# Turning ten units' last keys by VectorE blocks and a DRAM trip in place of TensorE, in a gated linear attention followed by four experts

## The chip, the cores and the metric

The kernel runs on one core of one Trainium2 chip, as one program. The metric is device time in microseconds, from the first to the last instruction of a launch as the device reports it; lower is better. A core has a matrix engine (TensorE, called PE in the profile, with its weight loads as PEld), VectorE (DVE), ScalarE (ACT), GpSimd (POOL) and SyncE (SP), which here only issues DMAs. Each engine runs its own instructions in order, and engines wait for each other with semaphores. SBUF and PSUM are the on-chip memories, with 128 partitions each; DRAM is off the core.

## The reference

A recurrence over 768 tokens for 4 batches and 8 heads of width 48, and then a mixture of four two-layer experts on the rows it makes:

```python
state = np.zeros((B, H, D, D))                       # B, H, S, D = 4, 8, 768, 48
for t in range(S):
    state = alpha[:, :, t, :, None] * state + np.einsum('bhd,bhe->bhde', k[:, :, t], v[:, :, t])
    y[:, :, t] = np.einsum('bhd,bhde->bhe', q[:, :, t], state)
x = y.transpose(0, 2, 1, 3).reshape(B * S, H * D)    # 3072 x 384
p = domain_probs / (domain_probs.sum(-1, keepdims=True) + 1e-09)
for e in range(4):                                   # w1[e]: 384 x 1024, w2[e]: 1024 x 384
    out += p[:, e:e + 1] * (np.maximum(x @ w1[e], 0.0) @ w2[e])
```

All is float32.

## The kernel before

**Units.** The attention is cut into 24 units of 128 tokens: six blocks of tokens (`cb`) by four batches (`b`), numbered u = 0 to 23 with the batch running fastest. Tokens of a unit are worked on all at once. The decays inside a unit are applied in seven doubling levels: at level li, queries in the later half of each block of 2^(li+1) tokens are multiplied by the decay up to them, keys in the earlier half by the decay after them, and TensorE multiplies the two (`products`). After the seventh level the keys (`KTs[-1]`) carry the decay up to the unit's last token, and keys times values is what the unit adds to the running state `st` of its batch.

**Layouts.** In the working layout of keys, queries and decays, a partition is one of 64 padded channels of one of two heads of a pair, and along a partition lie 4 pairs by 128 tokens. From the third unit on (u >= 2), rows are loaded in runs so that VectorE can turn them into that layout with its own 32x32 block transposes (`turn`, L444). To multiply keys by values over tokens, the keys must lie with tokens on partitions. That last turn is made by TensorE, four 128x128 turns into PSUM (`turned`, L246), and a ScalarE copy from there into the tile `AT` (L658). `AT` held the decays until then and is free.

**Steps.** `attention(u)` is a generator of 17 steps:

| step | what is emitted |
|---|---|
| 0, 1, 2 | decays, keys and queries turned (L444); then the loads of the next unit's rows on SP's queue (L161, L165, L170, L171) |
| 3 to 10 | the levels: `copy_q` (ACT, L508), `next_q` and `next_k` (DVE, L515, L517, L529; ACT, L528), `products` (PE, L536), `take` (DVE, L546) |
| 11 | the products of the far half (PE, L602), the last products and takes, `next_k(6)` (DVE) |
| 12, 13 | the scores copied into `lat` (ACT: L615 in step 12, L619 in step 13) |
| 14 | `turn_keys`: the last keys turned (PE, L246) and copied to `AT` (ACT, L658) |
| 15 | `result`: scores times values and queries times state (PE, L641, into `yps`), copied out by ACT and DVE (L653, L654) |
| 16 | keys times values (PE, L672, into `sps`), the state updated (DVE, L680 to L683), the values of unit u + 2 loaded (SP, L165) |

**Experts.** Units form groups, the first of two units, the rest of four, save the last. For each group and expert, `up` runs the first layer (PE, L728, into `one`; ACT L730 and DVE L753 take it out of PSUM as two parts, a coarse one and the rest), and `down` the second (PE, L797, into `ops`; L821 or L823 adds it up). Weights are split in the same way once, written to DRAM (`kept`, L221) and read back piece by piece for each later group (L195 on SP's queue, 768 KB a piece, four pieces a layer). A first-layer piece is read again as soon as its last use has been emitted, and two of four second-layer pieces (`late`) after the first piece of the next `up`.

**Order.** The order on every engine is written out by hand. `deal` gives each step of each unit a due time within the time of the expert work before the unit's group is wanted; a unit takes two unit spaces (some 39 us each), so that two units are under way at once. The steps' places in that time are the fractions in `IN_PAIRS` for units 11 to 17 (`in_pairs`) and in `BEATS` for the others. `advance` adds up the costs that `cost` gives for the expert work, and emits the steps that have come due between two matmuls. Due times are not changed by what a step holds.

The names that matter below: `by_pairs` is 10, and `in_rows` holds for u >= 10. `keys()` gives a tile from the five buffers of `KT`. `NP` is 4 pairs, `P` 128, `QUAD` 32, `NTOK` 4, `D` 48, `HD` 64, `NCB` 6. `apart_` tells whether the key-value product is made for each head by itself (64 columns by 48) or for two heads at once (128 by 96, of which half is used). `dram` is a pool of DRAM tiles. `rv` holds the unit's values with tokens on partitions.

Of the kernel before, what the change touches and what calls it, by code (L numbers as in the profile page):

```python
# [10 lines left out]
F32 = mybir.dt.float32  # L11
# [9 lines left out]
def kernel(  # L21
# [11 lines left out]
    nc = tc.nc  # L33

    B, H, S, D = q.shape
    E, DM, F = moe_w1.shape
    P = 128
    NCB = S // P
    NP = H // 2
    HD = 64  # L40
    QUAD = 32
# [12 lines left out]
    n = np.arange(QUAD)[None, :]  # L54
# [10 lines left out]
    dram = ctx.enter_context(tc.tile_pool(name="dram", bufs=1, space=bass.MemoryType.DRAM))  # L65
# [32 lines left out]
    NTOK = P // QUAD  # L98
# [14 lines left out]
    def raw(u, nm):  # L113
        if nm == "v":
            return values[u % 2]
        return rows_of[nm][:, 0] if u >= in_runs else apart[nm] if u == 1 else early[nm]
# [16 lines left out]
    in_pairs = range(half + 2 * B + 1, half + 4 * B)  # L133
# [106 lines left out]
    def halves(t, m):  # L240
        return t.rearrange("p a (b two r) -> p a b two r", two=2, r=m)

    def turned(src):
        tp = ps.tile([P, NP, P], F32, name="tp", tag="w")
        for p in range(NP):
            nc.tensor.transpose(tp[:, p, :], src(p), ident)  # L246
        return tp
# [171 lines left out]

    def rest_of_first(AT, KT, rv):  # L420
        nc.scalar.copy(out=AT, in_=turned(lambda p: KT[:, p, :]))
        yield
        sps = ps.tile([P, NP, 2, D], F32, name="sps", tag="w")
        for p in range(NP):
            nc.tensor.matmul(sps[:, p], lhsT=AT[:, p], rhs=rv[:, 2 * p:2 * p + 2, :D], start=True, stop=True)
        for i in range(2):
            rows = slice(HD * i, HD * (i + 1))
            nc.vector.tensor_copy(out=sts[units[0][1]][rows, :, i, :], in_=sps[rows, :, i, :])
        load(2, "v")
        yield  # L430

    def attention(u):
        cb, b = units[u]
        ra, rk, rq, rv = (raw(u, nm) for nm in ("a", "k", "q", "v"))
        pair = lambda t: lambda p: t[:, 2 * p:2 * p + 2, :].rearrange("p b c -> p (b c)")
        keys = lambda: work.tile([P, NP, P], F32, name="KT", bufs=5)

        AT = work.tile([P, NP, P], F32, name="AT")
        QT = work.tile([P, NP, P], F32, name="QT")

        def turn(nm, out):
            t = runs_of[nm]
            t = bass.AP(tensor=t.tensor, offset=t.offset, ap=[list(t.ap[0]), [RUN, NP], [D, NTOK], [1, QUAD]])
            nc.vector.transpose(out=out.rearrange("p a (t n) -> p a n t", n=NTOK), in_=t)  # L444
# [7 lines left out]
        in_rows = u >= by_pairs  # L452
        if in_rows:
            nc.gpsimd.tensor_mul(rows_of["q"][:, 1], rows_of["q"][:, 1], rows_of["a"][:, 0])
        yield
        KT = keys()
        if u >= in_runs:
            nc.scalar.activation(out=AT, in_=AT, func=ACT.Copy, scale=ident_all[:, P + HALF:P + HALF + 1])  # L458
            turn("k", KT)
        else:  # L460
            nc.scalar.copy(out=KT, in_=turned(pair(rk)))
        dot = work.tile([P, 2, H], F32, name="dot", bufs=1)
# [33 lines left out]
        KTs = [KT]  # L496
# [23 lines left out]
        def next_k(li):  # L520
            m = LEVELS[li]
            old = new = halves(KTs[li], m)
            if li == 0 and in_rows:
                KTs.append(KT)
            elif li + 1 < len(LEVELS):
                KTs.append(keys())
                new = halves(KTs[-1], m)
                nc.scalar.copy(out=new[:, :, :, 1, :], in_=old[:, :, :, 1, :])  # L528
            nc.vector.tensor_mul(new[:, :, :, 0, :], old[:, :, :, 0, :],  # L529
                                 spread(halved(decs[li])[:, :, :, 1], m))  # L530
# [11 lines left out]
        def take(li, scores):  # L542
            m = LEVELS[li]
            nb = HALF // (2 * m)
            mk = masks[:, li, :].rearrange("p (b r) -> p b r", r=m)
            nc.vector.copy_predicated(  # L546
                near.rearrange("p a (b two r) -> p a b two r", two=2, r=m)[:, :, :, 1, :],
                mk.unsqueeze(1).broadcast_to([P, H, nb, m]),
                scores.rearrange("p a (b r) -> p a b r", r=m))
# [50 lines left out]
        for r in range(NP // 2):  # L600
            for s in range(2):
                nc.tensor.matmul(far[HALF * s:HALF * (s + 1), r],  # L602
                                 lhsT=KTs[6][:, 2 * r + s, :HALF], rhs=qbs[6][:, 2 * r + s],
                                 start=True, stop=True)
# [3 lines left out]
        take(4, bank[:, 0])  # L608
        take(5, bank[:, 1])
        next_k(6)  # L610
        yield
        parts = lat.rearrange("p (r s i) c -> p r s i c", s=2, i=2)
        for s in range(2):
            rows = slice(HALF * s, HALF * (s + 1))
            nc.scalar.copy(out=parts[:HALF, :, s, :, HALF:], in_=far[rows])  # L615
        yield
        for s in range(2):
            rows = slice(HALF * s, HALF * (s + 1))
            nc.scalar.copy(out=lat[rows, :, rows], in_=near[rows])  # L619
        KT = KTs[-1]  # L620
        yield

        st = sts[b]
# [30 lines left out]
            nc.vector.tensor_sub(low, yps, top.bitcast(F32))  # L654

        def turn_keys():
            if cb < NCB - 1:
                nc.scalar.copy(out=AT, in_=turned(lambda p: KT[:, p, :]))  # L658


        for step in (turn_keys, result) if u >= half else (result, turn_keys):
            step()
            yield

        if cb < NCB - 1:
            KB = AT
            apart_ = u + 1 in in_pairs
            sps = ps.tile([P, NP, 1 if apart_ else 2, D], F32, name="sps", tag="w")
            for p in range(NP):
                for i in range(2) if apart_ else [slice(0, 2)]:  # L670
                    rows = slice(HD * i, HD * (i + 1)) if apart_ else slice(0, P)
                    nc.tensor.matmul(  # L672
                        sps[rows, p], lhsT=KB[:, p, rows],
                        rhs=rv[:, 2 * p + i, :D] if apart_ else rv[:, 2 * p:2 * p + 2, :D],
                        start=True, stop=True)
            for i in range(2):
                rows = slice(HD * i, HD * (i + 1))
                old, add = st[rows, :, i, :], sps[rows, :, 0 if apart_ else i, :]
                if cb == 0:
                    nc.vector.tensor_copy(out=old, in_=add)  # L680
                else:
                    nc.vector.tensor_mul(old, old, decs[-1][rows].broadcast_to([HD, NP, D]))
                    nc.vector.tensor_add(old, old, add)  # L683
# [159 lines left out]
    def deal():  # L843
# [14 lines left out]
        for gis in [*([gi] for gi in range(1, LAST - 1)), [LAST - 1, LAST]]:  # L858
# [6 lines left out]
            for k in range(n):  # L865
                u = sum(map(len, groups[:gi])) + k
                end = due - (n - 1 - k) * space
                begin = max(end - 2 * space, ends[-2])
                ends.append(end)
                run = attention(u)  # L870
                pairs = u in in_pairs
                beats = [0.0, *(IN_PAIRS if pairs else BEATS)]
                due_at = {-1: begin, **{j: begin + (end - begin) * beats[j + 1] for j in (7, 11, 16)}}
                for ahead, j in TOGETHER if pairs else ():
                    if (u > in_pairs[0] or j == 11) and abs(times[-1][ahead] - due_at[j]) < space / 6:
                        due_at[j] = times[-1][ahead]

                marks = sorted(due_at)
                times.append([])
                for lo, hi in zip(marks, marks[1:]):  # L880
                    times[-1] += [due_at[hi] if j == hi else
                                  due_at[lo] + (due_at[hi] - due_at[lo]) * (beats[j + 1] - beats[lo + 1])
                                  / (beats[hi + 1] - beats[lo + 1]) for j in range(lo + 1, hi + 1)]

                for j, ahead in ((6, 13), (12, 15)):
                    if times[:-1]:
                        times[-1][j] = max(times[-1][j], times[-2][ahead] + 0.5)
                events += [(time, u, run) for time in times[-1]]
# [8 lines left out]
    with tc.manual_schedule():  # L897
# [22 lines left out]
        def fill(times, n=P):  # L920
            for _ in range(times):
                nc.tensor.matmul(idle[:, :n], lhsT=zeros[:, :P], rhs=zeros[:, :n], start=True, stop=True)

        runs = [None, attention(1)]
        fill(7)
        runs[0] = first_unit(fill, runs[1])
# [56 lines left out]
```

## Time and profile before

| what | us |
|---|---|
| median of 3 runs (lowest to highest) | 1003.51 (1002.51 to 1006.27) |
| the profiled execution: time, span of its instructions | 1003.91, 1002.1 |
| DVE block turn L444, 128x512, mean of one (AT, KT, QT) | 1.10, 1.10, 1.10 |
| PE turn L246, 128x128, mean of one | 0.273 |
| ACT copy L658, 128x512 out of PSUM, mean of one | 0.585 |
| DMA to landing, median: `w<-kept` 768 KB, `sa` 88 KB, `out_dram<-acc` 192 KB | 6.8, 2.3, 2.3 |

The granted TensorE clock is 0.999 of full speed over the span. Landing times are counted from the issue, so a DMA behind others in its queue shows a longer one. On PE, f32 matmuls leave two records each, matmuls in the reduced f32 format (`fp32r`) one.

The units' places in the span, from the timeline: far products (step 11) of units 10, 11, 12, 17, 18, 19 start at 325.9, 351.6, 392.2, 588.2, 643.2 and 676.6 us; their key-value products (step 16) at 351.1, 391.7, 430.9, 625.3, 664.8 and 697.8 us. The first layer of an expert starts at 317.6, 359.4, 398.6, ... 632.8, 672.4 us, the second at 338.2, 379.7, 418.9, ... 651.0, 694.4 us.

### The profile page before, as it was taken

Reading aid. Unit: us, or ns where it says so; the run is one execution under the profiler, and the core shown is the slowest. Engines: PE = TensorE matmul, PEld = TensorE weight load, DVE = VectorE, ACT = ScalarE, POOL = GpSimd, SP = SyncE. Lnnn points to the kernel's source line nnn. Section 1 sums busy time; section 2 is a strip of 40 time slices with the busy share of each in tenths; the row PEclk is TensorE's granted clock in tenths of the full one; section 3 lists DMA queues with packets and bytes.
Section 4 is the critical chain, followed back from the end, with each engine's and each line's share of the span. In section 5 each row is a group of like instructions: output and inputs, shape, how many; then the busy total and the mean of one; then the engine's idle time right before and its main releaser. Section 6 shows DMA issues by size and latency. Waiting matters only on the chain.

```text
span 1002.1 us, 20402 instructions
## 1 busy us (share of the span) xinstructions
PE 979.5 (98%) x8244; PEld 869.9 (87%) x8244; DVE 572.2 (57%) x1188; ACT 407.2 (41%) x886; POOL 51.8 (5%) x94
## 2 busy tenths in 40 slices
PE   8799899999999999999999999999999999999998
PEld 7667678988989889889899899898898999999997
DVE  5688878476776555665645646756676521222222
ACT  5667656454452542523533413345344322111111
POOL 2000001000011000000000000000000000000000
PEclk9999999999999999999999999999999999999999
DMA  8898989595976774955946849759767405060611
GB/s 182 269 290 216 297 279 361 165 315 138 320 213 215 253 231 135 294 191 167 323 137 210 253 153 261 245 138 301 233 174 252 158 1 217 36 220 34 222 47 32
DMA packets 182798, 204.95 MB, mean 205 GB/s; under 512 B 110608, under 2 KB 159120, under 8 KB 182704
## 3 DMA queue, kind: packets, MB, share of 16 engines
q1 hardware_dynamic: 176240, 173.79, 57.8%
q0 software_dynamic: 6016, 29.49, 7.5%
q8 instruction: 65, 1.06, 0.4%
q10 hardware_dynamic: 448, 0.36, 0.1%
q14 instruction: 29, 0.24, 0.1%
HBM read 173.72 MB, written 29.88 MB: 203 GB/s over the span
## 4 chain that ended last, share of the span: by engine, by line
PE 84%; DVE 7%; ACT 4%; issue 2%; DMA 2%; SPq 1%; POOL 1%; DVEq 0%; ACTq 0%; POOLq 0%
PE ops L797 38%; PE one L728 34%; PE sc L536 5%; PE yps L641 3%; ACT qb L508 2%; PE sps L672 1%; DVE w L220 1%; DVE near L546 1%; PE far L602 1%; DMA raw<-in_moe_w_dram 1%; PE one L722 1%; DVE QT L515 1%; PE tp L246 1%; DVE QT L444 1%; DVE hT L753 1%
## 5 line engine op out<-in xcount | busy, mean ns | idle before, releaser
L797 PE MATMUL ops<-w,hT 128*128 128x384 f32 x2112 | 381.3, 338 | 1.0 <-DVE hT L753 1.0
L797 PEld LDWEIGHTS ops<-w,hT 128*128 128x128 f32 x2112 | 364.2, 188 | 5.9 <-DVE hT L753 2.6
L728 PE MATMUL one<-xT,w 128*128 128x512 f32 x1440 | 338.5, 393 | 0.0
L728 PEld LDWEIGHTS one<-xT,w 128*128 128x128 f32 x1440 | 268.7, 188 | 57.8 <-DVE hT L753 0.5
L730 ACT ACTIVATE hT<-one 128x512 fp32r<-128x512 f32 (+1 forms) x192 | 108.0, 563 | 312.5 <-PE one L728 310.8
L753 DVE SCALAR_TENSOR_TENSOR hT<-one,hT 128x512 fp32r<-128x512 f32 (+1 forms) x192 | 121.8, 643 | 112.8 <-ACT hT L730 112.7
L508 ACT COPY qb<-QT 64x256 f32<-64x256 f32 x294 | 119.7, 407 | 76.5 <-DVE QT L515 62.2
L515 DVE TENSOR_TENSOR QT<-QT,AT 128x256 f32<-128x256 f32 x158 | 68.0, 430 | 86.6 <-ACT qb L508 85.4
L823 DVE SCALAR_TENSOR_TENSOR acc<-ops,p_all,acc 128x384 f32<-128x384 f32 x66 | 38.1, 611 | 91.1 <-PE ops L797 91.0
L546 DVE COPY_PREDICATED near<-masks,sc 128x256 f32<-128x256 uint8 x124 | 63.7, 514 | 15.3 <-PE sc L536 13.2
L536 PEld LDWEIGHTS sc<-qb,KT 128*64 128x64 f32 x1984 | 63.2, 138 | 8.5 <-issue 5.0
L536 PE MATMUL sc<-qb,KT 128*64 128x64 f32 x1984 | 67.6, 223 | 2.5 <-ACT qb L508 2.5
L529 DVE TENSOR_TENSOR KT<-KT,AT 128x256 f32<-128x256 f32 x161 | 67.2, 418 | 0.9 <-PE tp L246 0.9
L528 ACT COPY KT<-KT 128x256 f32<-128x256 f32 x124 | 51.5, 415 | 3.9 <-DVE KT L529 1.0
L797 PE MATMUL ops<-raw,hT 128*128 128x384 f32 x128 | 45.0, 493 | 0.9 <-DVE AT L444 0.9
L722 PE MATMUL one<-xT,raw 128*128 128x256 f32 (+1 forms) x240 | 45.1, 340 | 0.4 <-ACT xT L416 0.4
L517 DVE TENSOR_TENSOR AT<-AT 128x256 f32<-128x256 f32 (+1 forms) x138 | 40.5, 293 | 4.7
L722 PEld LDWEIGHTS one<-xT,raw 128*128 128x128 f32 x240 | 38.1, 191 | 5.2 <-ACT xT L416 0.6
L458 ACT ACTIVATE AT<-AT,ident 128x512 f32<-128x512 f32 x22 | 15.9, 724 | 63.9 <-DVE AT L444 62.9
L797 PEld LDWEIGHTS ops<-raw,hT 128*128 128x128 f32 x128 | 23.1, 190 | 15.0 <-DMA raw<-in_moe_w_dram 1.5
L641 PE MATMUL yps<-lat,rv 128*32 128x128 f32 x736 | 33.1, 273 | 2.6 <-ACT lat L619 2.6
L728 PE MATMUL one<-raw,w 128*128 128x256 f32 x288 | 34.6, 279 | 0.0
(115 smaller groups left out, 640.8 us busy)
## 6 DMA issues: line engine op xcount, KB each, us to landing
w<-kept SPq DMA_DIRECT2D x144, 768.0 KB, 6.8
kept<-w POOLq DMA_DIRECT2D x32, 768.0 KB, 7.3
raw<-in_moe_w_dram SPq DMA_DIRECT2D x48, 384.0 KB, 7.6
rv<-in_v_dram SPq DMA_DIRECT2D x24, 192.0 KB, 3.3
rk<-in_k_dram SPq DMA_DIRECT2D x22, 192.0 KB, 3.8
rq<-in_q_dram SPq DMA_DIRECT2D x22, 192.0 KB, 7.5
out_dram<-acc POOLq DMA_DIRECT2D x22, 192.0 KB, 2.3
sa<-in_alpha_dram SPq DMA_DIRECT2D x44, 88.0 KB, 2.3
```

Source lines behind the costliest of these rows:

```text
L508: nc.scalar.copy(out=qb[rows, :, i, :].rearrange("p a (b r) -> p a b r", r=m), in_=qv[rows])
L515: nc.vector.tensor_mul(qv, qv, spread(dv[:, :, :, 0], m))
L528: nc.scalar.copy(out=new[:, :, :, 1, :], in_=old[:, :, :, 1, :])
L529: nc.vector.tensor_mul(new[:, :, :, 0, :], old[:, :, :, 0, :], spread(halved(decs[li])[:, :, :, 1], m))
L536: nc.tensor.matmul(out[HALF * s:HALF * (s + 1), 2 * p:2 * p + 2, :], lhsT=KTs[li][:, p, HALF * s:HALF * (s + 1)], rhs=qbs[li][:, p, :, QUA ...
L546: nc.vector.copy_predicated(near.rearrange("p a (b two r) -> p a b two r", two=2, r=m)[:, :, :, 1, :], mk.unsqueeze(1).broadcast_to([P, H, ...
L641: nc.tensor.matmul(yps[QUAD * j:QUAD * (j + 1), c, :], lhsT=lhsT, rhs=rhs, start=begins, stop=ends)
L722: nc.tensor.matmul(one, lhsT=w[:, kc], rhs=xTs[gi][:, 0, kc, lo:hi], start=(kc == 0), stop=(kc == KC - 1))
L728: nc.tensor.matmul(one, lhsT=w[:, of_w, kc], rhs=x_part(gi, of_x)[:, kc, :n], start=k == 0, stop=k == len(turns) - 1)
L730: nc.scalar.activation(out=parts[0], in_=one, func=ACT.Relu)
L753: nc.vector.scalar_tensor_tensor(out=low, in0=x, scalar=0.0, in1=top.bitcast(F32), op0=ALU.max, op1=ALU.subtract)
L797: nc.tensor.matmul(sums[slot], lhsT=h, rhs=w, start=(n == begins[slot]), stop=(n == ends[slot]))
```

## The change

For units 10 to 19 (`moved`: in rows, and not the last block of tokens, which adds to no further state) the turn of the last keys leaves TensorE. In step 11, VectorE turns each 32x32 block of the last keys in place within its quadrant of 32 partitions, into another buffer of `KT`, blocks set in the order of tokens' block, pair, channel. In step 12, SP writes this tile to a DRAM tile `over`, 256 KB, 2 KB for each partition and token block. In step 13, SP reads it back with four DMAs, one for each block of 32 tokens, into 32 partitions of `AT` each, in runs of 512 bytes. Now tokens lie on partitions; along a partition lie four blocks of channels by four pairs by 32 channels. `turn_keys` in step 14 does nothing for these units. In step 16 the key-value product takes 16 matmuls with 32 columns each, for each pair and each block of channels, in place of 8 with 64 columns (units 10 to 16) or 4 with 128 columns for two heads at once (units 17 to 19). The update of the state is the same.

```diff
@@ -608,16 +608,27 @@
         next_k(6)
+        moved = in_rows and cb < NCB - 1
+        if moved:
+            by_quad = keys().rearrange("x a n -> x (a n)").rearrange("x (t a c) -> x t a c", a=NP, c=QUAD)
+            nc.vector.transpose(out=by_quad.rearrange("x t a c -> x a t c"),
+                                in_=KTs[-1].rearrange("x a (t n) -> x a t n", n=QUAD))
         yield
         parts = lat.rearrange("p (r s i) c -> p r s i c", s=2, i=2)
         for s in range(2):
             rows = slice(HALF * s, HALF * (s + 1))
             nc.scalar.copy(out=parts[:HALF, :, s, :, HALF:], in_=far[rows])
+        if moved:
+            over = dram.tile([P, NTOK, NP * QUAD], F32, name="over", bufs=2)
+            nc.sync.dma_start(out=over, in_=by_quad.rearrange("x t a c -> x t (a c)"))
         yield
         for s in range(2):
             rows = slice(HALF * s, HALF * (s + 1))
             nc.scalar.copy(out=lat[rows, :, rows], in_=near[rows])
         KT = KTs[-1]
+        for t in range(NTOK if moved else 0):
+            nc.sync.dma_start(out=AT[QUAD * t:QUAD * (t + 1)],
+                              in_=over.rearrange("(g r) t n -> t r g n", r=QUAD)[t])
         yield
@@ -654,7 +665,7 @@
         def turn_keys():
-            if cb < NCB - 1:
+            if cb < NCB - 1 and not moved:
                 nc.scalar.copy(out=AT, in_=turned(lambda p: KT[:, p, :]))
@@ -664,9 +675,15 @@
         if cb < NCB - 1:
             KB = AT
-            apart_ = u + 1 in in_pairs
+            apart_ = u + 1 in in_pairs or moved
             sps = ps.tile([P, NP, 1 if apart_ else 2, D], F32, name="sps", tag="w")
-            for p in range(NP):
+            for p in range(NP if moved else 0):
+                for g in range(P // QUAD):
+                    at = QUAD * (NP * g + p)
+                    nc.tensor.matmul(sps[QUAD * g:QUAD * (g + 1), p, 0],
+                                     lhsT=KB.rearrange("x a n -> x (a n)")[:, at:at + QUAD],
+                                     rhs=rv[:, 2 * p + g // 2, :D], start=True, stop=True)
+            for p in range(0 if moved else NP):
                 for i in range(2) if apart_ else [slice(0, 2)]:
                     rows = slice(HD * i, HD * (i + 1)) if apart_ else slice(0, P)
                     nc.tensor.matmul(
```

## The prediction

> **What bounds the kernel now.** The page first: which engine is full, then what ended the chain of work. Then the busy time by stretch, to see whether TensorE (PE) is full where the changed units run.
>
> ```profile
> span 1002.1 us, 20402 instructions
> PE 979.5 (98%) x8244; PEld 869.9 (87%) x8244; DVE 572.2 (57%) x1188; ACT 407.2 (41%) x886; POOL 51.8 (5%) x94
> ...
> PE 84%; DVE 7%; ACT 4%; issue 2%; DMA 2%; SPq 1%; POOL 1%; DVEq 0%; ACTq 0%; POOLq 0%
> ```
> ```profile
> 398.60:437.80 39.20, 39.20 (x334) 35.31 (x333) 24.17 (x51) 14.95 (x32) 1.10 (x1) 1.00 0.68 210
> 632.80:672.40 39.60, 39.60 (x325) 35.71 (x324) 28.49 (x62) 18.63 (x41) 3.12 (x4) 1.00 0.73 210
> 672.40:713.80 41.40, 41.40 (x367) 37.14 (x366) 28.23 (x58) 15.87 (x34) 1.02 (x1) 1.00 0.82 234
> ```
> The second fence is the view of stretches (PE, PEld, DVE, ACT, POOL busy, clock, DMA share): three rounds of one expert's first and second layer. PE is busy in every microsecond at full clock, VectorE (DVE) 60 to 72%, ScalarE (ACT) under half, the DMA engines 68 to 82%. So whatever PE no longer does here is won, whatever makes PE wait is lost, and work on DVE or ACT costs only if PE comes to wait for it. From 320 to 720 us, where units 10 to 19 end (counting from 0), PE waited once for another engine: 0.5 us at 337.5, for ACT's qb.
>
> **Removed: four turns on PE and one ACT copy a unit.** The timeline of PE around unit 19:
>
> ```profile
> 684.68 4.06 PE L728 MATMUL one<-xT,w 128*128 128x512 f32 x17
> ...
> 688.58 0.60 PE L246 MATMUL tp<-ident,KT 128*128 128x128 f32 x4
> ...
> 688.94 2.32 PE L728 MATMUL one<-xT,w 128*128 128x512 f32 x9
> ...
> 694.40 3.58 PE L797 MATMUL ops<-w,hT 128*128 128x384 f32 x19
> ...
> 697.82 1.02 PE L672 MATMUL sps<-rv,AT 128*128 128x96 f32 x8
> ...
> 698.63 0.60 PE L797 MATMUL ops<-w,hT 128*128 128x384 f32 x2
> ```
> Matmuls overlap, so the cost is read between starts. The last L728 before the turns starts at 684.68 + 4.06 - 0.39 (its own duration) = 688.35, the next at 688.94: 0.59 us, where neighbours lie (4.06 - 0.39)/16 = 0.23 apart. The four turns cost 0.36 us; ten units, **3.6 us**. The ACT copy L658 (0.59 us) goes too; ACT has room, so it wins nothing.
> The Trainium skill (TensorE: Matmul & The Clock Gate, Part 4: PE-mode transpose) gives about 275 ns for one turn inside a kernel, and the row here agrees as a duration (273 ns). Forty times that would save 11 us; between starts the trace shows a third of it, so the trace decides. The skill (VectorE: DVE Perf Modes, Rules for kernel authors) also sends a 128x128 turn to TensorE when PSUM is a good place for it, because VectorE turns 32x32 blocks only: a rule against this change, which needs the DRAM trip for that reason.
>
> **Changed on PE: the key-value product (sps).** Units 17 to 19 now issue 4 matmuls of 128 columns by 96 (8 records, as f32 counts twice). Last L797 starts at 694.40 + 3.58 - 0.34 = 697.64, the next at 698.63: 0.99, less the usual 0.18, is 0.81 us. Units 10 to 16 already split them into 8 (16 records of 64 columns by 48), 0.77 us from the last L797 to the matmul behind, less 0.18 = 0.59. New are 16 matmuls (32 records) of 32 columns by 48, neighbours on different columns. Nearest row: the first unit's y, also 32 columns wide, 52 weight loads in 0.95 us, so 32 in 0.58, like the 0.55 that the 16 take now. The far row is yps, 56 records in 1.46 us between first and last start (they move 128, not 48): 32 in 0.83. I take +0.05 for seven units and -0.2 for three: -0.25 in all; bounds -0.7 (as the 16 now) and +2.8. Four DMAs now fill AT where one ACT copy did, so PE waits for up to three more semaphores; the one L246 shows on PE's sequencer takes 51 ns, so 0 to 1.5 us over ten units, taken as 0.7, half, as some will run ahead. **PE saves 3.6 + 0.25 - 0.7, about 3.1 us** (bounds 4.3 and -0.7).
>
> **Added on DVE:** one block turn, 1.09 us by the three rows of L444 (same 128x512), between next_k(6) and what follows. Queued behind it are the next unit's turns and the subtractions L753, which free the PSUM of the first layer. Cover: DVE idles 11 us and more in each round above, and L753 works for the products one to two back with four PSUM banks (about 2 us each). Without cover it would cost 1.1 x 10 = 11 us. I take nothing. KT now goes through its five buffers seven times a unit; each buffer's last reader lies half a unit back: nothing.
>
> **Added on SP's queue: five DMAs a unit,** 256 KB out, then four of 64 KB in that must wait until the store has landed. Each costs SP some 0.4 us to issue; 0.5 MB a unit, at 768 KB in 1.8 us (below), is about 1.2 us of DMA time in a 39 us round: room. The wait is the question: SP issues in order, its DMAs land in order, and 768 KB weight pieces are ahead. In units 11 to 17 PE has some 24 us from lat's second copy (L619, the place of the new loads) to sps: unit 12's store comes behind two second-layer pieces (400.3 and 400.9, landing up to 408.3), its loads behind row loads that SP gets through at 416, so AT lands at about 420 and sps starts at 430.9. The next second-layer pieces land 1 us later, at 413 and 416, for use from 419. Nothing there.
> Units 10, 18 and 19 have the wider steps (BEATS) and little room. SP around unit 19:
>
> ```profile
> 675.40 3.01 SPq L195 DMA_DIRECT2D w<-kept  x5
> 678.51 2.47 SPq L161 DMA_DIRECT2D sq<-in_q_dram  x4
> 682.82 0.39 SPq L165 DMA_DIRECT2D rq<-in_q_dram  x1
> 684.74 5.08 SPq L170 DMA_DIRECT2D rq<-in_q_dram  x2
> 690.06 0.95 SPq L171 DMA_DIRECT2D ra<-in_alpha_dram  x1
> 691.12 2.41 SPq L195 DMA_DIRECT2D w<-kept  x3
> ```
> ```profile
> DMA to landing us min/median/max: 5.6/6.1/6.6
> ```
> ACT runs L615 (the store's place) at 683.1 and L619 (the loads' place) at 685.6. PE is through first-layer piece 1 at about 682 and piece 2 at about 686, so the store comes behind the first L195 of the last group and the loads ahead of the second. But SP is late: it reaches that group only at 691.1, held by landings of its earlier DMAs (L170's two issues take 5 us; in the waits of SP's queue L170 stands behind w<-kept 16 times, 18.4 us). The second fence is the landing of its first two pieces: 691.1 + 5.6 = 696.7, and 691.9 + 6.6 = 698.5. So 768 KB take 1.8 us and 256 KB 0.6: the store lands at 697.3. Then four loads, like L161's of 88 KB (starts 1.4 us from first to last, landing 2.1 later): AT is whole at 697.3 + 3.5 = 700.8. sps would start at 697.82 - 0.36 = 697.5. **PE waits 3.4 us.** If the store must run wholly after the piece, as the output's 192 KB do (2.3 us, scaled 3.1), it lands at 699.8 and PE waits 5.8; if the store passes the piece, 0.
> The Trainium skill (DMA: Bandwidth & Descriptors, Anatomy of one DMA) gives 2.0 us plus bytes over 436 GB/s, most of it the confirmation of the last write, and worst towards HBM: 2.6 us for the store, an estimate. Put wholly behind the piece, that makes PE's wait 5.3; no row here shows a store behind loads.
> Unit 18 by the same sum: the piece ahead is issued at 654.6, lands 5.2 later at 659.8, store 660.4, AT 663.9, sps due at 664.4: 0.5 to spare. Unit 10: piece 338.2 + 7.4 = 345.6, store 346.2, AT 349.7, sps due 350.7: 1.0 to spare. With the late store (2.5 more) they wait 2.0 and 1.5. What SP holds back behind the loads (first-layer pieces 2 and 3 of the next expert) is wanted 20 us later.
>
> **Sum:** -3.1 + 3.4 = +0.3 us on the profiled execution's 1003.9 (span 1002.1). That execution lies 0.4 above the median 1003.5, so I forecast 1003.8.
>
> **Rivals.**
> A, no wait: unit 19's store goes out earlier, or lands beside the piece. For: PE's position is read from ACT copies. Against: every DMA of SP around there lands in the order of issue. Only the savings remain: 1000.4, at best 999.2.
> B, slower: the store's landing, late by more than the 0.6 us. Each further microsecond costs unit 19 one, unit 18 after 0.5, unit 10 after 1.0; the change is a loss from a stall of 3.1. With 2.5 more: 5.8 + 2.0 + 1.5 = 9.3 us of waiting, 1009.7. For: SP's queue is full there; against: landings of one ring overlap.
> C, slower: DVE's block turn gets on the path. For: the one wait at 337.5 hangs on DVE and ACT in turn. Against: DVE's idle time. 1003.8 + 11 = 1014.8.
> D, faster: the turns cost PE their duration, 273 ns x 40 = 10.9 rather than 3.6: 996.5. Against: starts.
>
> **Chances:** forecast 0.62, A 0.16, B 0.13, C 0.05, D 0.04. A measurement of this kernel tells about 0.5% (5.0 us) from no change. The forecast and A lie inside, but for a tenth of the forecast's case whose waits go past 5; D and a little of A are faster (0.06), B, C and that tenth slower (0.24), same 0.70. The range goes from A's best, 999.2, to just short of B's, 1009: it leaves out C, D and part of B.
>
> **What would show it.** Right: no L658 and no tp in ten units, 160 matmuls 32 columns wide on L672's successor, some 50 DMAs more on SP, PE idle over 3 us once, just before unit 19's sps near 695 us, released by a DMA of AT, none in units 11 to 17. Wrong: waits before many sps, PE waiting for L753 or for weight pieces, or a store that lands more than 1 us behind the piece ahead of it.

## The result, and the profile after

| | before | changed |
|---|---|---|
| median (lowest to highest) of 8 runs each, us | 1004.68 (1002.51 to 1007.90) | 1000.40 (997.86 to 1002.28) |
| ratio, 95% interval | | 0.9955 [0.9944, 0.9966] |
| the profiled execution: time, span | 1003.91, 1002.1 | 1002.28, 1000.5 |

The changed kernel is 0.45% faster, 4.3 us between the medians; the forecast was 0.3 us slower. The profiled execution of the changed kernel is the slowest of its eight. The page of the changed kernel, the lines that answer to those shown of before:

```profile
span 1000.5 us, 20763 instructions
PE 976.8 (98%) x8388; PEld 866.4 (87%) x8388; DVE 580.6 (58%) x1198; ACT 402.5 (40%) x876; POOL 51.4 (5%) x94
...
PE 83%; DVE 7%; ACT 5%; issue 2%; DMA 1%; SPq 1%; DVEq 0%; POOL 0%; ACTq 0%; POOLq 0%
```

The bound has not moved: PE is still full. The view of stretches for the same three rounds (time, then busy PE, PEld, DVE, ACT, POOL, clock, DMA share):

```profile
399.37:438.13 38.76, 38.76 (x345) 34.86 (x345) 25.40 (x52) 14.45 (x31) 1.02 (x1) 1.00 0.73 226
630.61:669.76 39.15, 39.05 (x345) 34.82 (x345) 29.13 (x63) 18.20 (x40) 3.13 (x4) 1.00 0.75 229
669.76:712.29 42.53, 40.75 (x385) 36.21 (x385) 28.62 (x59) 15.38 (x33) 1.00 (x1) 1.00 0.81 237
```

The first round is 0.44 us shorter than before (39.20), and PE is busy throughout. The second is 0.45 us shorter (39.60 before), with 0.1 us of idle time: unit 18's product waited 0.10 us for its keys. The third is 1.1 us longer (41.40 before) and holds 1.8 us of PE's idle time: unit 19's wait. PE's timeline there:

```profile
691.74 3.11 PE L814 MATMUL ops<-w,hT 128*128 128x384 f32 x17
696.63 0.55 PE L683 MATMUL sps<-rv,AT 128*32 128x48 f32 x32 [1.78 <-DMA AT<-over]
697.11 1.14 PE L814 MATMUL ops<-w,hT 128*128 128x384 f32 x5
```

So the forecast wait is there, in its place and with its cause, but of 1.8 us. SP's timeline, and in a second fence the landing of its L195 at 687.17 and of its store L623:

```profile
686.29 0.78 SPq L171 DMA_DIRECT2D ra<-in_alpha_dram  x1
687.17 1.25 SPq L195 DMA_DIRECT2D w<-kept  x1
688.51 0.38 SPq L623 DMA_DIRECT2D over<-KT  x1
693.22 1.75 SPq L630 DMA_DIRECT2D AT<-over  x4
695.06 0.85 SPq L195 DMA_DIRECT2D w<-kept  x2
```
```profile
DMA to landing us min/median/max: 5.4/5.4/5.4
...
DMA to landing us min/median/max: 4.7/4.7/4.7
```

The order is the one foretold: one weight piece, store, loads, two pieces. The piece lands at 692.5, the store at 693.2, 0.6 us behind it, and AT is whole at 694.53 + 1.96 = 696.5, 3.3 us behind the store.

**A finer count than the medians.** No kernel of this study lets PE wait between 345 and 640 us, so the starts of the layers on PE's timeline repeat from one execution to the next within 0.01 us, once they are counted from the first layer near 318 us, the last one that the change can't reach. The time until there is untouched code and differs by several microseconds between executions (316.3 to 322.1 us in the 14 profiles of this study). All sums below are by this count, in us against the profile of before; a round has two layers, and the column `after` is the first profile of the changed kernel.

| up to | after | noturn | narrow | turns2 | again1 | again2 | sooner |
|---|---|---|---|---|---|---|---|
| units 10 to 16, end (613 us) | -3.57 | -3.57 | +0.03 | +3.52 | -3.58 | -3.57 | -4.28 |
| unit 17, product done (633) | -3.79 | -3.79 | -0.19 | +3.52 | -3.80 | -3.79 | -4.50 |
| unit 18, product done (672) | -4.29 | -4.46 | -0.41 | +3.96 | -4.32 | -4.29 | -5.17 |
| unit 19, turn's place passed (694) | -4.75 | -4.92 | -0.41 | +4.40 | -4.78 | -4.75 | -5.63 |
| unit 19, product done (714) | -3.13 | -5.15 | -0.63 | +4.38 | -2.91 | -3.90 | -5.86 |

The row of 613 us has eight units' turns in it (unit 17's too), and seven products. Every changed unit wins 0.44 to 0.46 us where its turn stood, whichever layer that is, and 0.0 us at its product, or 0.22 for units 17 to 19. From 714 us to the last layer (989 us) no column changes any more.

### The profile page after: what moved, and what is told of

It is laid out like the page before. It is cut to its first block, busy times and chain, and to the rows that moved or that the text cites. A ratio compares the mean times of both kernels' runs of the same rounds, so it can differ in the third digit from the quotient of the medians.

```text
span 1000.5 us, 20763 instructions
## 1 busy us (share of the span) xinstructions
PE 976.8 (98%) x8388; PEld 866.4 (87%) x8388; DVE 580.6 (58%) x1198; ACT 402.5 (40%) x876; POOL 51.4 (5%) x94
## 4 chain that ended last, share of the span: by engine, by line
PE 83%; DVE 7%; ACT 5%; issue 2%; DMA 1%; SPq 1%; DVEq 0%; POOL 0%; ACTq 0%; POOLq 0%
PE ops L814 38%; PE one L745 33%; PE sc L536 4%; PE yps L652 3%; ACT qb L508 2%; PE far L602 1%; DVE near L546 1%; DVE w L220 1%; PE one L739 1%; DVE QT L515 1%; DVE hT L770 1%; PE tp L246 1%; DVE KT L529 1%; ACT KT L528 1%; DVE QT L444 1%
```

## The experiments

**The trip left out (noturn).** The store, the loads and VectorE's turn are left out, and nothing takes their place: `AT` still holds the decays. The narrow products stay.

```diff
-        if moved:
-            by_quad = keys().rearrange("x a n -> x (a n)").rearrange("x (t a c) -> x t a c", a=NP, c=QUAD)
...
-            nc.sync.dma_start(out=over, in_=by_quad.rearrange("x t a c -> x t (a c)"))
...
-        for t in range(NTOK if moved else 0):
...
```

> Leaves out the turn of the last keys of units 10 to 19 altogether: no block turn, no DRAM trip, and the narrow products read the decays that AT holds. Theory (VectorE's turn and the five DMAs are hidden): 4.7 us faster than before counted from the same layer start, the same as a changed kernel without its one wait, within 0.2 us. Rival (the added DVE work or DMA traffic costs PE something in each unit): 1 us or more faster than early19.

Measured: 5.15 us won by the count, 0.45 more than was expected, ratio 0.9949 [0.9933, 0.9965]. Up to unit 17 it agrees with the changed kernel and with early19 (below) to 0.01 us in every layer. So VectorE's turns and the DMAs cost PE nothing, nor do the semaphores of four DMAs. All that the trip costs is what the waits cost: 0.17 us at unit 18 (a wait of 0.10), and 1.85 at unit 19 (a wait of 1.78; the changed kernel loses 1.62 there where noturn wins 0.23). The sign of the rival, 1 us faster than early19, is there too, but it comes from early19's waits at units 18 and 19.

**The narrow products alone (narrow).** TensorE turns, ACT copies, and the 16 products read AT's channels in plain order. The lines shown differ from the changed kernel; its VectorE turn, store and loads are left out too.

```diff
-            if cb < NCB - 1 and not moved:
+            if cb < NCB - 1:
...
-                                     lhsT=KB.rearrange("x a n -> x (a n)")[:, at:at + QUAD],
+                                     lhsT=KB[:, p, QUAD * g:QUAD * (g + 1)],
```

> Undoes the turn (PE turns the keys, ACT copies them) and keeps the 16 narrow products. Theory: the products cost PE the same in units 10 to 16 (+0.0) and 0.2 us less in units 17 to 19, so 0.6 to 0.7 us faster than before; the turns keep the rest (4.1 us). Rival (narrow products make the gain): 2 us or more faster than before. The prediction had -0.25 us without semaphore waits.

Measured: -0.63 by the count, 0.22 in each of units 17 to 19 and +0.00 in the others; the runs' ratio, 1.0001 [0.9989, 1.0012], can't tell that from nothing. What is left of the 5.15 is the turns: 4.52, or 0.45 a unit and not 0.36.

**The turns doubled (turns2),** in the kernel before:

```diff
-                nc.scalar.copy(out=AT, in_=turned(lambda p: KT[:, p, :]))
+                tp = turned(lambda p: KT[:, p, :])
+                for p in range(NP if in_rows else 0):
+                    nc.tensor.transpose(tp[:, p, :], KT[:, p, :], ident)
+                nc.scalar.copy(out=AT, in_=tp)
```

> The kernel before with TensorE's four turns of units 10 to 19 made twice, eight a unit. Theory now (a turn takes 0.109 us of PE, and the reading of 0.36 for four stopped one matmul too soon): +0.43 us a unit, 4.3 to 4.4 in all. Rival 1 (four turns cost 0.36 and a fixed late start of 0.09 follows them): +0.36 a unit, 3.6 in all. Rival 2 (a turn costs its duration, 273 ns): +1.1 a unit, 10.9 in all.

Measured: +0.44 in every unit, 4.38 in all. PE's timeline at unit 19 shows it: the second four start 0.43 us behind the first.

```profile
692.82 0.60 PE L246 MATMUL tp<-ident,KT 128*128 128x128 f32 x4
693.25 0.60 PE L660 MATMUL tp<-ident,KT 128*128 128x128 f32 x4
```

A turn costs 0.109 us (4.38 over 40 turns); of something fixed behind them, 0.45 less 0.44, 0.01 us at most is left. The prediction had stopped at the first product behind the turns. In the trace of before that one product is the longer one, 0.48 us where its neighbours take 0.39:

```profile
688.94 0.48 PE L728 MATMUL one<-xT,w 128*128 128x512 f32 x1
```

It starts early, while the last turn is still under way, and the 0.09 us come out of its end: the second product starts 0.32 us behind the first, where 0.23 is usual.

**Unit 19 left alone (not19), units 18 and 19 left alone (not1819).**

```diff
-        moved = in_rows and cb < NCB - 1
+        moved = in_rows and u < 19          # not1819: u < 18
```

> Unit 19 keeps its turn on PE and its 128-column product; units 10 to 18 are changed. Theory (each unit's turns cost PE 0.45 us, a late start behind them included; unit 19's wait gives 1.6 us back): no wait of PE on AT from DMA anywhere, the first layer that starts behind unit 19's product about 1.0 us sooner than in the changed kernel when both are counted from the first layer that starts at 319 us; over all 4.05 us sooner than before by the same count. Rival (the wait is moved, not lost): PE waits 1 us or more elsewhere and nothing is won on the changed kernel.

Measured: -3.36 where -4.05 was expected, ratio 0.9957 [0.9942, 0.9971]. Unit 19's wait is gone, but unit 18 now waits 1.04 us (0.10 in the changed kernel's first profile): half of what the rival says. Up to unit 18 the two programs are the same.

> Units 18 and 19 keep TensorE's turns and their wide products; units 10 to 17 are changed. Theory: no wait at all, 8 x 0.45 + 0.2 = 3.8 us faster than before by the same count, every run. Rival (the waits move to unit 17 or 10): a wait of PE on AT shows there and less than 3 us are won.

Measured: -3.80, no wait on AT, ratio 0.9948 [0.9931, 0.9966], as the theory said, in the one execution that was profiled. By the runs, leaving two units out costs nothing that shows.

**The changed kernel again (again1, again2).**

> The changed kernel once more. Theory (the wait hangs on where the DMA stream stands when unit 18's and 19's store joins it): the 0.44 to 0.45 us won by each of units 10 to 16 comes out again to 0.01 us, the waits of units 18 and 19 differ from those of the first profile (0 and 1.8 us) by up to 2 us. Rival (the wait is set by the program): the same waits to 0.2 us.

> A third look at the changed kernel, with what was expected of the second.

Measured: -2.91 and -3.90, with waits of 2.03 and 1.01 us before unit 19's product, of 0.08 and 0.11 before unit 18's, and the same 0.44 to 0.46 elsewhere. The wait's size belongs to the execution, the gain to the program.

**The store one step sooner, unit 19 (early19).**

```diff
+        if moved and u == 19:               # right behind the block turn, in step 11
+            over = dram.tile([P, NTOK, NP * QUAD], F32, name="over", bufs=2)
+            nc.sync.dma_start(out=over, in_=by_quad.rearrange("x t a c -> x t (a c)"))
...
-        if moved:
+        if moved and u != 19:
```

> Unit 19's store is issued one step sooner, right behind its block turn, so that it goes out ahead of the weight piece that held it. Theory: the store lands before that piece, AT is whole about 2 us or more before the product, no wait, and the whole is 1.6 us faster than the changed kernel, 4.7 us faster than before (counted from the same layer start). Rival (SP, waiting for VectorE, now holds the weight pieces): the piece behind the store is issued later than PE releases it and PE waits at a later layer; no gain.

This one missed. The profiled execution, the slowest of twelve, waited 0.53 us at unit 18, where nothing is changed yet, and 3.12 us at unit 19; by the count -0.03 us is left, not -4.7; ratio 0.9964 [0.9946, 0.9982]. SP's timeline there:

```profile
690.88 1.07 SPq L171 DMA_DIRECT2D ra<-in_alpha_dram  x1
692.05 0.57 SPq L618 DMA_DIRECT2D over<-KT  x1
692.71 0.38 SPq L195 DMA_DIRECT2D w<-kept  x1
694.65 1.74 SPq L633 DMA_DIRECT2D AT<-over  x4
```

The store did pass the piece and landed at 694.6, but now the loads stood behind it: the piece landed 6.2 us after its issue, at 698.9, and the loads 4.6 to 5.2 us after theirs, up to 701.1. AT was whole 2.2 us behind the piece, not 4.0 as in the changed kernel; but in this execution SP issued the piece 5.4 us before the product was due, where it was 7.7 in the changed kernel's first profile. So how much of the wait is the new order, and what passing the piece with half of the trip is worth, one profile does not tell. The twelve runs can't be told from the changed kernel's.

**Store and loads a step later (late).** Both move down by one step, the store behind L619.

```diff
         KT = KTs[-1]
-        for t in range(NTOK if moved else 0):
...
+        if moved:
+            over = dram.tile([P, NTOK, NP * QUAD], F32, name="over", bufs=2)
...
         def turn_keys():
...
+            for t in range(NTOK if moved else 0):
...
```

> Store and loads one step later each (behind the second copy into lat, and in the place of the turn). Theory (AT lands some 3.3 us behind the store, which lands 0.6 us behind the weight piece issued ahead of it): unit 18's store now stands behind the expert's last first-layer piece, so its product waits 1 us or more longer than in the changed kernel; unit 19's wait stays within 2 us of what it was, as its loads now stand behind one more piece; units 11 to 17 still do not wait. Rival (the trip has several microseconds to spare and the one wait was a chance of that run): no wait at units 18 and 19, or one no longer than before.

Measured: -2.25, waits of 1.22 us at unit 18 and 1.49 at unit 19, no others. Unit 18's wait grew by 1.1 us over that of the changed kernel's first profile, as the theory had it; not19 shows that the execution alone can do nearly as much.

**All five DMAs from POOL (pool).**

```diff
-            nc.sync.dma_start(out=over, in_=by_quad.rearrange("x t a c -> x t (a c)"))
+            nc.gpsimd.dma_start(out=over, in_=by_quad.rearrange("x t a c -> x t (a c)"))
...
-            nc.sync.dma_start(out=AT[QUAD * t:QUAD * (t + 1)],
+            nc.gpsimd.dma_start(out=AT[QUAD * t:QUAD * (t + 1)],
```

> All five DMAs of the trip are issued by POOL instead of SP, so they no longer stand behind weight pieces in SP's queue. Theory (the waits come from that queue's order and nothing else of the trip costs PE anything): no wait on AT, 5.1 us faster than before counted from the first layer at 319 us, as without the trip. Rival (the DMA engines are shared, and POOL's own issues are slow): AT still lands behind the pieces and PE waits 1 us or more before units 18 or 19's product.

Measured: ratio 0.9959 [0.9944, 0.9975]. In the profile, the slowest of ten runs, unit 19 does not wait, but unit 18 does, 2.64 us, and -0.92 is left, as the rival has it. Its four loads and their landing, and PE behind them:

```profile
L630 POOL DMA_DIRECT2D AT<-over x4: 548/554/567, 654.0 to 655.7; - x4
...
DMA to landing us min/median/max: 2.7/5.8/8.2
```
```profile
664.14 0.74 PE L683 MATMUL sps<-rv,AT 128*32 128x48 f32 x32 [2.64 <-DMA AT<-over]
```

Issued beside weight pieces on SP's queue, the small loads take up to 8.2 us: they land between 656.7 and 663.9, the two pieces beside them at 659.3 and 664.1. The Trainium skill (DMA: Bandwidth & Descriptors, Issuing engines are not separate DMA queues) says that DMAs of all engines run on the same 16 DMA engines and interleave; this trace agrees.

**The three units' steps sooner (sooner).** Steps 11 to 13 of units 10, 18 and 19 move up, step 16 stays.

```diff
+    SOONER = [*BEATS[:11], 0.65, 0.675, 0.71, 0.87, 0.94, 1.0]
...
-                beats = [0.0, *(IN_PAIRS if pairs else BEATS)]
+                beats = [0.0, *(IN_PAIRS if pairs else SOONER if u in (10, 18, 19) else BEATS)]
```

> The due times of steps 11, 12 and 13 of units 10, 18 and 19 come sooner (0.65, 0.675, 0.71 of the unit's time in place of 0.69, 0.75, 0.8), so that SP gets unit 19's loads ahead of two first-layer pieces and unit 18's ahead of the last one. Theory (the waits come from these three units' short way from store to product): AT lands 2 us or more before every product, no wait on it, all of 5.1 us won counted from the first layer at 319 us. Rival (step 11 sooner makes PE wait for ACT's or VectorE's part of that step): waits of PE on ACT or VectorE near 640 and 673 us, and less than 4 us won.

Measured: -5.86, no wait on AT, median 999.00, ratio 0.9945 [0.9927, 0.9963] to before. AT landed 1.6 us ahead of unit 18's product and 1.3 ahead of unit 19's, less than the 2 us expected. SP and PE at unit 19:

```profile
684.64 0.94 SPq L624 DMA_DIRECT2D over<-KT  x1
687.39 1.74 SPq L631 DMA_DIRECT2D AT<-over  x4
689.24 1.32 SPq L196 DMA_DIRECT2D w<-kept  x3
```
```profile
689.78 2.24 PE L815 MATMUL ops<-w,hT 128*128 128x384 f32 x12
691.96 0.55 PE L684 MATMUL sps<-rv,AT 128*32 128x48 f32 x32
692.44 0.79 PE L815 MATMUL ops<-w,hT 128*128 128x384 f32 x3
```

Now the whole trip goes out ahead of the three pieces, and the product starts right behind the layer's. Of the 5.86, 0.71 come from unit 10: they are there at 338 us, before its turn's place, and 0.5 of them is PE's old wait for ACT at 337.5, which is gone. By the count this beats the changed kernel by 2.0 to 3.0 us; the runs (0.9945 and 0.9955 with overlapping intervals) are too coarse to show it, and one profile does not tell how often a wait is left.

**Units 18 and 19 by the other plan (pairs20):** `in_pairs` ends two units later.

> Units 18 and 19 take the steps of units 11 to 17 (IN_PAIRS), which leave some 24 us from the loads' place to the product. Theory: no wait on AT and about 5 us won by the same count, as in sooner; the split into steps by itself moves nothing on PE. Rival (the other steps of these units, or those of units 20 and on, no longer fit between the layers): new waits behind 640 us, and less is won than in sooner.

Measured: -5.15, no wait, ratio 0.9950 [0.9936, 0.9964]. As expected; between sooner and this one lies only unit 10's part.

## Why the prediction was wrong, by its own steps

Both terms of the sum were mis-sized. PE's saving was put at 3.1 us and is 5.15: the turns cost 0.9 us more, the semaphores 0.7 less and the products 0.4 less than was taken. Unit 19's wait was put at 3.4 us and was 1.0 to 2.0. The mechanism, turns off a full PE against one wait in SP's queue, was right.

- **PE as the bound, DVE and DMAs hidden:** right. Layers agree to 0.01 us with and without the trip up to 633 us.
- **The four turns at 0.36 us, 3.6 in all:** mis-sized, 0.45 and 4.5 (noturn less narrow; 0.44 in turns2). The rule, cost between starts, was right and rival D's 273 ns wrong, but the reading ended one product early.
- **The product, -0.25:** it was -0.63. That 32 records of 32 columns take what 16 of 64 do was the lower bound given, and the right one. (The upper bound, +2.8, is 0.83 less 0.55 for all ten units, though units 17 to 19 started from a dearer product.)
- **Semaphores, +0.7:** 0. The 51 ns waits are on PE's sequencer (20 of them now), ahead of the work.
- So PE saves 5.15 us and not 3.1; the stated bound of 4.3 was too tight, since the turns' 3.6 was given no uncertainty.
- **Unit 19's wait, 3.4 us** (700.8 less 697.5 is 3.3): place, cause, the store's 0.6 us behind the piece and the loads' 3.3 us (3.5 foretold) were right. The size was not: 1.8, 2.0 and 1.0 us in three executions. The term that failed is the time at which the piece ahead lands. The trace of before had it 0.8 us before the product's due time (696.7 against 697.5); in the changed kernel's first profile it landed 692.5 against 694.85, the product's start without its wait of 1.78: 2.3 us before, and in again1 and again2 2.1 and 3.1. Store and loads took 4.0 us behind the piece in all three, so the wait follows this margin alone.
- **The prediction took that margin from one execution as if the program set it.** Five more profiles show the same piece with nothing of unit 19's trip in the queue. Less the 0.45 us of turns that the changed kernel no longer has (0.9 in turns2), it lands ahead of the product by 0.7 us in before, 0.6 in noturn, 2.5 in not19, 2.7 in not1819, 2.9 in narrow and 3.1 in turns2. In before, noturn, narrow and turns2 SP issues the same DMAs in the same order. By the same 4.0 us, noturn's margin would have made a wait of 3.4, an estimate: the forecast's wait fits two of the executions seen, and not most. What sets the margin stays open. The two small ones go with an `sa` issue on SP near 670 us that took 1.4 to 1.6 us, where 0.4 is usual, but not1819 had a like delay at an `rk` issue and kept its margin, and no experiment tried it by itself.
- **Unit 18 with 0.5 to spare, unit 10 with 1.0:** near. Unit 18 waits 0.10 us in the first profile, 0.53 in early19 and 1.04 in not19, with the same program up to there; unit 10 never waits.
- **The sum:** -5.15 + 0.17 + 1.85 = -3.13, where -3.1 + 3.4 = +0.3 stood. Both errors point the same way. Rival A's time, 1000.4, came out by luck: the wait was there, the saving was larger, and the median of before that it started from had since risen from 1003.5 to 1004.7. The runs' ratio stands for 3.4 to 5.6 us; the three profiles give 2.9 to 3.9, its lower end. What the rest is stays open. The first 318 us differ by more than that, the waits of the executions that were not profiled are not known, and only one profile of the kernel before was at hand.

## What to carry to other kernels

Read what an interruption of a matmul stream costs from the last regular start ahead of it to the second regular start behind it, or from when the next stage begins: the first one behind can start early and run long. A transfer's round trip behind bulk loads is a margin of that execution and not a number of the program: look for its spread over several executions. Here moving the whole trip ahead of the bulk transfers left no wait in its profile; moving its first half, or all of it to another queue, left waits in theirs. Where PE is full, compare starts of stages between profiles from the last point that the change can't reach: that told 0.2 us where the runs' medians told 1 to 2.

## What was not expected of the hardware

**A wait of 2.6 us cost 4.2.** Behind PE's longest waits the granted clock fell to half for one stretch of 3.4 us. The view of stretches of the kernel with POOL's DMAs, around its wait that ended at 664.1:

```profile
650.00:661.00 11.00, 11.00 (x150) 10.48 (x149) 4.32 (x10) 4.65 (x12) 3.21 (x5) 1.00 1.02 271
664.30:667.70 3.40, 3.40 (x41) 3.28 (x33) 2.43 (x7) 0.81 (x2) 0.00 (x0) 0.51 0.30 58
668.00:672.00 4.00, 4.00 (x25) 4.00 (x25) 3.43 (x6) 0.73 (x1) 0.00 (x0) 1.00 0.48 115
```

The same came behind early19's wait of 3.12 us, which cost 4.5:

```profile
700.90:704.30 3.40, 3.04 (x39) 2.96 (x40) 2.01 (x7) 0.51 (x2) 0.00 (x0) 0.50 0.90 323
```

It came behind none of the six waits of 1.0 to 2.0 us; those cost 0.06 to 0.13 us more than their length. So pool's unit 18 lost 4.2 us: 2.64 of waiting and about 1.6 of slow matmuls (half the clock for 3.4 us is worth at most 1.7, an estimate). The Trainium skill (TensorE: Matmul & The Clock Gate, Part 1: The HAM clock gate) lets the clock fall after a whole idle window of about 3.4 us. The slow stretch has that length here, but 2.64 us of idle time was enough.

**The added block turn was cheaper than the old ones.** It takes 0.71 us, the older ones 1.09, for the same 128x512, by the view of lines with shapes apart:

```profile
L444 DVE STREAM_TRANSPOSE AT<-sa 128x512 f32<-128x512 f32 x22 | 23.9, 1087 | 0.0
L614 DVE STREAM_TRANSPOSE KT<-KT 128x512 f32<-128x512 f32 x10 | 7.1, 712 | 0.3
```

The old ones read runs of 32 out of a longer row and write single elements four apart; the new one reads and writes blocks of 32 elements in a row. Which of the two sides matters was not tried.
